# Batch-wide softmax steps on ScalarE and GpSimd, with the maximum and the reciprocal halved on VectorE

## The chip, the cores and the metric

The kernel runs on one core of a Trainium2 chip. A core has five engines that run side by side, each in the order of its own queue: TensorE (PE in the profile, its weight loads PEld), VectorE (DVE), ScalarE (ACT), GpSimd (POOL) and SyncE (SP), which issues the DMAs. The metric is the device time of one execution in microseconds (us); lower is better.

## What is computed

Every token has 8 heads with 7 taps each. A softmax over the 7 taps weighs 7 neighbouring rows of x; the result feeds a feed-forward layer whose activation is h·cos(h).

```python
w = weight_gen - np.max(weight_gen, axis=-1, keepdims=True)
w = np.exp(w)
w = w / (np.sum(w, axis=-1, keepdims=True) + 1e-09)
out = np.einsum('bshk,bskhg->bshg', w, x_unf)      # 8 x 4096 tokens, 192 wide
h = out.reshape(B * S, D) @ w_in                    # 192 -> 2048
return (h * np.cos(h)) @ w_out                      # 2048 -> 192
```

## The kernel before

**Tiling.** A partition holds 256 consecutive tokens (rows). A batch is 4 rows on each of 128 partitions, 512 tokens; there are 64 batches. The 2048 hidden columns are cut into 16 chunks, and a step of the main loop (line 678) handles a pair of chunks of one batch: 8 pairs to a batch, 512 pairs in all, counted by `i`. One softmax (line 263) covers 16 rows, four batches, so it recurs every 32 pairs. I call these 32 pairs a round, and the place in it `p` = i mod 32.

**One pair.** TensorE computes `h` (lines 428 and 445) and, eight pairs behind, the second layer into `acc` (line 519). The cosine goes back and forth: ScalarE L455 rounds `h` to whole turns, VectorE L459 takes the fraction, ScalarE L463 takes the sine, VectorE L466 forms h·cos(h), ScalarE L473 and VectorE L477 split it into a high and a low part for TensorE. There are three `h` buffers; L477 is the last reader of one. `acc` has one buffer. ScalarE empties it with L541 every fourth pair (p = 3, 7, 11, ...), and copies transposed rows out of it with L535 and L536 two pairs from there (p = 1, 5, 9, ...). In every even pair ScalarE also converts transposed rows (L385), and GpSimd finishes them with L387 and L390.

**GpSimd's other work.** For each batch `attention` (line 331) multiplies and adds the seven neighbours: L344 makes a product, L359 adds it to `xa`. Its steps run ahead in the background, two a pair. TensorE transposes the finished `xa` two batches before it is needed, from p = 6, 14, 22 and 30 on (L407). L550 adds the two halves of an output.

**The softmax.** `softmax(..., early=False)` is a generator; line 750 advances it one step at the end of each pair, starting at p = 9 with the load of the taps. VectorE finds the maximum (L276, p = 10); GpSimd subtracts and clips (L278, L285, p = 11). `powers` (line 196) then forms the exponential without ScalarE's exponential table, and does it in two halves of 448 elements a partition: ten ScalarE instructions (L206, twice L214, L224, L228, each for two halves) at p = 14, 15 and in each of p = 18 to 25, and twelve GpSimd instructions (L209 and L211; L217, L219 and L221; L231). At p = 27 GpSimd sums the taps (L190, L193, L297), at p = 29 VectorE takes the reciprocal (L303), and at p = 30 GpSimd multiplies (L309).

**What sets the order.** Each engine's order is the order in which the code emits instructions; nothing reorders them. The tile framework adds the waits between engines.

Of the kernel before, what the change touches and what calls it, by code (L numbers as in the profile page):

```python
# [11 lines left out]
F32 = mybir.dt.float32  # L12
# [4 lines left out]
AF = mybir.ActivationFunctionType  # L17
ALU = mybir.AluOpType
AX = mybir.AxisListType
# [26 lines left out]
LN_2 = math.log(2.0)  # L46
ONE_BITS = float(127 * 2 ** 23)
# [3 lines left out]
def tile_softmax_conv_then_cos_ffn(  # L51
# [8 lines left out]
    nc = tc.nc  # L60
# [36 lines left out]
    early = const.tile([P, 1], F32, name="early")  # L97
# [89 lines left out]
    def add_taps(t, out):  # L187
        three_ = work.tile([P, RW * H, K], F32, name="side", bufs=1)
        three = three_[:, 0:t.shape[1], 0:3]
        nc.gpsimd.tensor_tensor(out=three, in0=t[:, :, 0:3], in1=t[:, :, 3:6], op=ALU.add)  # L190
        old = three[:, :, 0]
        for more in (three[:, :, 1], three[:, :, 2], t[:, :, 6]):
            nc.gpsimd.tensor_tensor(out=out, in0=old, in1=more, op=ALU.add)  # L193
            old = out

    def powers(t):

        (a1, b1), (a2, b2) = EXP_A
        n = t.shape[1]
        whole_ = work.tile([P, RW * H, K], I32, name="whole", bufs=1)  # L200
        side_ = work.tile([P, RW * H, K], F32, name="side", bufs=1)
        cut = (slice(0, n // 2), slice(n // 2, n))
        t, whole, side = ([v[:, c] for c in cut] for v in (t, whole_, side_))

        def near(k):
            nc.scalar.activation(out=whole[k], in_=t[k], func=AF.Identity, scale=1.0 / LN_2)  # L206

        def rest(k):
            nc.gpsimd.tensor_scalar(  # L209
                out=side[k], in0=whole[k], scalar1=-LN_2, scalar2=1.0, op0=ALU.mult, op1=ALU.mult)  # L210
            nc.gpsimd.tensor_tensor(out=t[k], in0=side[k], in1=t[k], op=ALU.add)  # L211

        def square(k, to, a):
            nc.scalar.activation(out=to[k], in_=t[k], func=AF.Square, bias=a, scale=0.5)  # L214

        def quartic(k):
            nc.gpsimd.tensor_scalar(  # L217
                out=side[k], in0=side[k], scalar1=b1, scalar2=1.0, op0=ALU.add, op1=ALU.mult)
            nc.gpsimd.tensor_scalar(  # L219
                out=t[k], in0=t[k], scalar1=b2, scalar2=1.0, op0=ALU.add, op1=ALU.mult)  # L220
            nc.gpsimd.tensor_tensor(out=t[k], in0=t[k], in1=side[k], op=ALU.mult)  # L221

        def power(k):
            nc.scalar.activation(  # L224
                out=whole[k], in_=whole[k], func=AF.Relu, bias=ONE_BITS, scale=2.0 ** 23)

        def again(k):
            nc.scalar.activation(out=t[k], in_=t[k], func=AF.Square)  # L228

        def product(k):  # L230
            nc.gpsimd.tensor_tensor(out=t[k], in0=t[k], in1=whole[k].bitcast(F32), op=ALU.mult)  # L231

        near(0)
        yield
        near(1)
        rest(0)
        yield
        rest(1)
        yield
        yield  # L240
        square(0, side, a1)
        yield
        square(0, t, a2)
        yield
        square(1, side, a1)
        quartic(0)
        yield
        square(1, t, a2)
        yield
        power(0)  # L250
        quartic(1)
        yield
        power(1)
        yield
        again(0)
        yield
        again(1)
        product(0)
        yield
        product(1)  # L260
        yield

    def softmax(r0, r1, eng, early=True, to=None):
        n = (r1 - r0) * H
        if r0 == 0:
            t = const.tile([P, n, K], F32, name="taps0")
        else:
            tile_ = work.tile([P, RW * H, K], F32, name="taps")
            t = tile_[:, 0:n, :]
        nc.sync.dma_start(out=t.rearrange("p a k -> p (a k)"), in_=g_v[:, :, r0 * H * K:r1 * H * K])  # L270
        for b in range(r0 // R, r1 // R):
            taps[b] = t.rearrange("p (r h) k -> p r h k", h=H)[:, b * R - r0:(b + 1) * R - r0]
        yield
        top_ = work.tile([P, RW * H], F32, name="top", bufs=1)
        top = top_[:, 0:n]
        nc.vector.tensor_reduce(out=top, in_=t, axis=AX.X, op=ALU.max)  # L276
        yield
        eng.tensor_tensor(  # L278
            out=t, in0=t, in1=top.unsqueeze(2).broadcast_to([P, n, K]), op=ALU.subtract)
        if early:  # L280
            yield
            nc.scalar.activation(out=t, in_=t, func=AF.Exp)
            yield
        else:
            eng.tensor_scalar(  # L285
                out=t, in0=t, scalar1=0.0, scalar2=EXP_LEAST, op0=ALU.min, op1=ALU.max)
# [10 lines left out]
        (nc.vector if early else nc.gpsimd).tensor_scalar(  # L297
            out=den, in0=den, scalar1=1e-9 / (1.0 if early else EXP_UNIT), scalar2=TWO_PI,
            op0=ALU.add, op1=ALU.mult)
        yield  # L300
        if not early:
            yield
        nc.vector.reciprocal(out=den, in_=den)  # L303
        yield
        m = 0 if to is None else to.shape[1]
        if m:
            eng.tensor_tensor(
                out=to, in0=t[:, 0:m], in1=den[:, 0:m].unsqueeze(2).broadcast_to([P, m, K]), op=ALU.mult)
        eng.tensor_tensor(  # L309
            out=t[:, m:], in0=t[:, m:], in1=den[:, m:].unsqueeze(2).broadcast_to([P, n - m, K]),  # L310
            op=ALU.mult)
        ready.update(range(r0 // R, r1 // R))
# [80 lines left out]
    def transpose_all(b):  # L393
        xa = mixed[b]
        tr = ps_h.tile([P, 2, CT], F32, name="h")
        for part in range(2):
            for r in range(R):
                nc.tensor.transpose(tr[:, part, r * P:(r + 1) * P], xa[:, r, columns(part)], ident)
        transposed.add(b)
        return tr  # L400
# [207 lines left out]
    own = own.rearrange("p a b -> p (a b)")  # L608
    own_taps = own[:, 0:RV * H * K].rearrange("p (n k) -> p n k", k=K)
    sm0 = softmax(0, R, nc.vector, to=own_taps)  # L610
    next(sm0)
    load_rows(0)
    w_b0 = w_in_b(0)
    w_a0 = w_in_a(0, 256)
    sm1 = softmax(R, 3 * R, nc.gpsimd)
    next(sm1)
    load_rows(1)
    w_a1 = w_in_a(256, 768)
    sm2 = softmax(3 * R, 3 * R + RW, nc.gpsimd)
    next(sm2)  # L620
    load_weights(-1)
# [56 lines left out]
    for i in range(N + LAG + 1):  # L678
# [48 lines left out]
        if whole is not None:  # L727
            t = work.tile([P, 2, CT], F32, name="part", bufs=2)
# [65 lines left out]
```

## Time and profile before

| | us |
|---|---|
| median of 3 runs (lowest, highest) | 2228.36 (2226.72, 2228.66) |
| profiled execution, its own time | 2226.02 |
| profiled execution, span from first to last instruction | 2224.2 |
| DVE busy | 1900.0 (85%) |
| ACT busy | 1869.2 (84%) |
| POOL busy | 2015.8 (91%) |

A group row of the profile reads: line, engine, operation, output<-inputs, shapes (partitions x elements), count, then busy time in us and the mean of one in ns, then the idle time of the engine ahead of it and what ended that. A timeline row reads: start in us from the span's start, duration in us, engine, line, operation; where the engine stood idle ahead of it, that time and its releaser follow in brackets. A wait row reads: who waited for whom, total us, how often, longest us. A row of the windows reads: stretch, its length, then busy us of PE, PEld, DVE, ACT and POOL with instruction counts, then the granted TensorE clock.

### The profile page before, as it was taken

What the parts mean: (1) busy time and instruction counts of PE and PEld (TensorE: products, weight loads), DVE (VectorE), ACT (ScalarE), POOL (GpSimd) and SP (SyncE); (2) the same over time, 40 slices, a digit from 0 to 9 for tenths busy, and PEclk for the clock granted to TensorE, in tenths of its full rate; (3) what the DMA queues carried; (4) which work ended last, traced back from release to release, by engine and by line L of the source; (5) the groups of instructions that cost most, each with busy time, mean ns of one, the idle gap of its engine ahead of it and who ended that gap; (6) DMA issues with size and microseconds to landing.
All of it is one profiled execution on the core that took longest, in us unless ns stands there. A gap on an engine that the chain in (4) does not pass through costs nothing.

```text
span 2224.2 us, 62220 instructions
## 1 busy us (share of the span) xinstructions
PE 2160.8 (97%) x26552; PEld 1677.8 (75%) x26552; DVE 1900.0 (85%) x1638; ACT 1869.2 (84%) x2352; POOL 2015.8 (91%) x1778
## 2 busy tenths in 40 slices
PE   5699999999999999999999999999999999999998
PEld 3477777777777777777777777777777777777777
DVE  6888888888888888888888888888888888888886
ACT  4688888988888898888988888888888988888885
POOL 8999999999999999999999999999999999989830
PEclk7899999999999999999999999999999999999999
DMA  7221221221221221211211221211212112212100
GB/s 176 49 48 34 56 48 38 51 48 39 51 56 30 59 48 30 60 43 43 52 42 45 48 50 39 56 42 40 56 34 56 48 34 56 48 36 48 30 16 19
DMA packets 53285, 105.67 MB, mean 48 GB/s; under 512 B 5791, under 2 KB 42135, under 8 KB 53007
## 3 DMA queue, kind: packets, MB, share of 16 engines
q1 hardware_dynamic: 53006, 101.69, 19.2%
q8 instruction: 208, 3.41, 0.7%
q14 instruction: 71, 0.57, 0.1%
HBM read 76.50 MB, written 25.17 MB: 46 GB/s over the span
## 4 chain that ended last, share of the span: by engine, by line
PE 55%; POOL 40%; issue 2%; ACT 1%; DVE 1%; DMA 0%; POOLq 0%; SPq 0%; ACTq 0%; DVEq 0%
PE acc L519 27%; PE h L445 17%; POOL xa L359 14%; POOL pr L344 11%; PE h L428 9%; POOL x_lo L390 3%; POOL part L550 2%; POOL taps L211 1%; POOL taps L221 1%; POOL taps L231 1%; POOL x_b L387 1%; POOL xa L344 1%; POOL den L193 1%; PE acc L407 1%; POOL side L209 1%
## 5 line engine op out<-in xcount | busy, mean ns | idle before, releaser
L459 DVE TENSOR_TENSOR turn<-h,turn 128x1024 f32<-128x1024 f32 x512 | 625.7, 1222 | 275.8 <-ACT turn L455 275.2
L519 PE MATMUL acc<-wo,ghi 64*128 64x384 f32 x8096 | 805.9, 336 | 1.8 <-DVE t L149 1.5
L519 PEld LDWEIGHTS acc<-wo,ghi 64*128 64x128 f32 x8096 | 724.5, 184 | 55.2 <-ACT part L541 10.8
L463 ACT ACTIVATE turn<-turn 128x1024 f32<-128x1024 f32 x512 | 541.7, 1058 | 216.3 <-DVE turn L459 216.3
L359 POOL TENSOR_TENSOR xa<-xa,pr 128x768 f32<-128x768 f32 (+1 forms) x384 | 698.6, 1819 | 1.7
L466 DVE SCALAR_TENSOR_TENSOR h<-h,turn 128x1024 f32<-128x1024 f32 x512 | 630.8, 1232 | 2.5 <-ACT turn L463 2.5
L477 DVE TENSOR_TENSOR glo<-h,ghi 128x1024 bf16<-128x1024 f32 x512 | 621.3, 1214 | 1.1 <-ACT ghi L473 1.1
L455 ACT ACTIVATE turn<-h 128x1024 int32<-128x1024 f32 x512 | 523.6, 1023 | 84.9 <-PE h L445 76.2
L344 POOL TENSOR_TENSOR pr<-xt,taps 128x768 f32<-128x768 f32 (+1 forms) x384 | 588.2, 1532 | 5.2
L473 ACT CAST ghi<-h 128x1024 fp32r<-128x1024 f32 x512 | 516.6, 1009 | 2.9 <-DVE h L466 1.3
L519 PE MATMUL acc<-wo_b,glo 64*128 64x192 bf16 x8096 | 462.5, 243 | 0.1
L519 PEld LDWEIGHTS <-glo 64*128 64x128 bf16 (+1 forms) x8128 | 318.1, 94 | 85.8 <-issue 67.7
L428 PE MATMUL h<-x_hi,wa_hi 64*128 64x512 f32 x1024 | 300.8, 583 | 0.0
L445 PE MATMUL h<-x_hi,wa_hi 64*128 64x512 f32 x1024 | 299.9, 582 | 0.0
L428 PE MATMUL h<-x_lo,wa_hi 64*128 64x512 bf16 x1024 | 199.0, 384 | 31.6 <-DVE glo L477 23.5
L445 PE MATMUL h<-x_hi,wb_hi 64*128 64x512 f32 x1024 | 204.2, 395 | 0.0
L428 PE MATMUL h<-x_b,wa_lo 64*128 64x512 bf16 x1024 | 196.7, 380 | 3.5 <-POOL wa_lo L155 3.5
L445 PE MATMUL h<-x_lo,wa_hi 64*128 64x512 bf16 x1024 | 196.0, 379 | 0.8
L445 PE MATMUL h<-x_b,wa_lo 64*128 64x512 bf16 x1024 | 196.2, 379 | 0.0
L445 PE MATMUL h<-x_lo,wb_hi 64*128 64x512 bf16 x1024 | 195.8, 379 | 0.0
L445 PE MATMUL h<-x_b,wb_lo 64*128 64x512 bf16 x1024 | 195.8, 378 | 0.0
L387 POOL TENSOR_SCALAR x_b<-x_hi 128x256 bf16<-128x256 f32 (+1 forms) x247 | 103.6, 420 | 93.0 <-ACT x_hi L385 90.6
(87 smaller groups left out, 2000.3 us busy)
## 6 DMA issues: line engine op xcount, KB each, us to landing
xt<-in_x_dram SPq DMA_DIRECT2D x62, 960.0 KB, 7.0
out_dram<-part SPq DMA_DIRECT2D x256, 96.0 KB, 2.2
taps<-in_weight_gen_dram SPq DMA_DIRECT2D x15, 448.0 KB, 4.5
raw<-in_moe_w_out_dram SPq DMA_DIRECT2D x8, 384.0 KB, 12.2
raw<-in_moe_w_in_dram SPq DMA_DIRECT2D x10, 256.0 KB, 11.1
xt<-in_x_dram SPq DMA_DIRECT2D x1, 768.0 KB, 10.0
xt<-in_x_dram SPq DMA_DIRECT2D x1, 540.0 KB, 5.5
raw<-in_moe_w_in_dram SPq DMA_DIRECT2D x4, 128.0 KB, 9.8
```

The source lines that it names most:

```text
L344: eng.tensor_tensor(out=dst.rearrange("p r (h g) -> p r h g", h=H), in0=xt[:, k + ra:k + rb, :].rearrange("p r (h g) -> p r h g", h=H), in ...
L359: eng.tensor_tensor(out=acc if k < K else xa, in0=acc, in1=old[:, ra:rb], op=ALU.add)
L387: nc.gpsimd.tensor_scalar(out=near[:, :, cs], in0=hi[:, :, cs].bitcast(F32), scalar1=1.0, scalar2=1.0, op0=ALU.mult, op1=ALU.mult)
L428: nc.tensor.matmul(h[:, q, :], lhsT=w[rs, chunk(pair, q)], rhs=v[rs, q, :], start=(m == 0), stop=False, skip_group_check=True)
L445: nc.tensor.matmul(h[:, 1 - q, :], lhsT=w[rs, cs], rhs=v[rs, q ^ middle, :], start=False, stop=(m == len(prods) - 1), skip_group_check=True)
L455: nc.scalar.activation(out=t.bitcast(I32), in_=hs[i], func=AF.Identity, bias=0.25, scale=1.0)
L459: nc.vector.tensor_tensor(out=t, in0=hs[i], in1=t.bitcast(I32), op=ALU.subtract)
L463: nc.scalar.activation(out=t, in_=t, func=AF.Sin, bias=SIN_BIAS, scale=SIN_SCALE)
L466: nc.vector.scalar_tensor_tensor(out=hs[i], in0=hs[i], scalar=TWO_PI, in1=turns.pop(i), op0=ALU.mult, op1=ALU.mult)
L473: nc.scalar.copy(out=hi, in_=hs[i])
L477: nc.vector.tensor_tensor(out=lo, in0=hs.pop(i), in1=hi.bitcast(F32), op=ALU.subtract)
L519: nc.tensor.matmul(to, lhsT=g[rs, n, t * P:(t + 1) * P], rhs=w[rs, fc, :], start=(lo == 0 and c == 0 and (k == 0 or whole and k == 1)), st ...
```

## The change

The halves in `powers` go: each of the five ScalarE and six GpSimd steps now handles all 896 elements in one instruction. ScalarE's steps stand at p = 14, 18, 20, 22 and 26, all even; empty steps (`wait`) keep them there. The maximum becomes two instructions, the first at p = 10 and the second at p = 11, just ahead of the subtraction. The sums move from p = 27 to p = 28. The reciprocal becomes two instructions at p = 30 and 31, and the multiplication stands at p = 32, which is p = 0 of the next round. The three startup softmaxes (`early=True`) keep one maximum and one reciprocal.

```diff
-        cut = (slice(0, n // 2), slice(n // 2, n))
-        t, whole, side = ([v[:, c] for c in cut] for v in (t, whole_, side_))
...
-        near(0)
-        yield
-        near(1)
-        rest(0)
-        yield
-        rest(1)
-        yield
-        yield
-        square(0, side, a1)
-        yield
-        square(0, t, a2)
-        yield
-        square(1, side, a1)
-        quartic(0)
...
+        whole, side = (v[:, 0:t.shape[1]] for v in (whole_, side_))
+        nc.scalar.activation(out=whole, in_=t, func=AF.Identity, scale=1.0 / LN_2)
+        yield
+        nc.gpsimd.tensor_scalar(
+            out=side, in0=whole, scalar1=-LN_2, scalar2=1.0, op0=ALU.mult, op1=ALU.mult)
+        nc.gpsimd.tensor_tensor(out=t, in0=side, in1=t, op=ALU.add)
+        yield
+        yield from wait(2)
+        nc.scalar.activation(out=side, in_=t, func=AF.Square, bias=a1, scale=0.5)
+        yield
+        yield from wait(1)
+        nc.scalar.activation(out=t, in_=t, func=AF.Square, bias=a2, scale=0.5)
...
+        nc.scalar.activation(out=whole, in_=whole, func=AF.Relu, bias=ONE_BITS, scale=2.0 ** 23)
+        nc.gpsimd.tensor_tensor(out=t, in0=t, in1=side, op=ALU.mult)
+        yield
+        yield from wait(3)
+        nc.scalar.activation(out=t, in_=t, func=AF.Square)
+        yield
+        nc.gpsimd.tensor_tensor(out=t, in0=t, in1=whole.bitcast(F32), op=ALU.mult)
...
-        nc.vector.tensor_reduce(out=top, in_=t, axis=AX.X, op=ALU.max)
-        yield
+        cut = (slice(0, n),) if early else (slice(0, n // 2), slice(n // 2, n))
+        for c in cut:
+            nc.vector.tensor_reduce(out=top[:, c], in_=t[:, c], axis=AX.X, op=ALU.max)
+            if early or c.start == 0:
+                yield
...
-        nc.vector.reciprocal(out=den, in_=den)
-        yield
+        for c in cut:
+            nc.vector.reciprocal(out=den[:, c], in_=den[:, c])
+            yield
```

The order on TensorE and SyncE stays as it was, so the DMAs do too. Lines from 303 on move up by 27 (L455 is L428 in the new file, L541 is L514), those between by 28 or 29.

The first place is ScalarE's queue at p = 18 to 20 of a round in the middle of the program. Before, one half-width step follows in every pair (`side` and `taps` are the operands of the exponential, `x_hi` the transposed rows, `part<-acc` the emptying of `acc`):

```order
L385 CAST x_hi<-xrow 128x2x128
L214 ACTIVATE side<-taps 128x448
L455 ACTIVATE turn<-h 128x1024
L473 CAST ghi<-h 128x1024
L463 ACTIVATE turn<-turn 128x1024
L541 COPY part<-acc 128x1024
L214 ACTIVATE taps<-taps 128x448
L455 ACTIVATE turn<-h 128x1024
L473 CAST ghi<-h 128x1024
L463 ACTIVATE turn<-turn 128x1024
L385 CAST x_hi<-part 128x2x128
L214 ACTIVATE side<-taps 128x448
```

After the change the same stretch holds two full-width steps:

```order
L358 CAST x_hi<-xrow 128x2x128
L213 ACTIVATE side<-taps 128x896
L428 ACTIVATE turn<-h 128x1024
L446 CAST ghi<-h 128x1024
L436 ACTIVATE turn<-turn 128x1024
L514 COPY part<-acc 128x1024
L428 ACTIVATE turn<-h 128x1024
L446 CAST ghi<-h 128x1024
L436 ACTIVATE turn<-turn 128x1024
L358 CAST x_hi<-part 128x2x128
L216 ACTIVATE taps<-taps 128x896
```

The step behind the copy out of `acc` is gone, and the step behind each conversion `x_hi` is twice as wide.

The second place is GpSimd's queue at p = 25 to 28, where `xa` for the transposes at p = 30 is finished. Before, five instructions of the sums stand ahead of the last addition to `xa`:

```order
L231 TENSOR_TENSOR taps<-taps,whole 128x448
L344 TENSOR_TENSOR pr<-xt,taps 128x768
L359 TENSOR_TENSOR xa<-xa,pr 128x768
L550 TENSOR_TENSOR part<-part 128x2x192
L190 TENSOR_TENSOR side<-taps 128x128x3
L193 TENSOR_TENSOR den<-side 128x128
L193 TENSOR_TENSOR den<-den,side 128x128
L193 TENSOR_TENSOR den<-den,taps 128x128
L297 TENSOR_SCALAR den<-den 128x128
L359 TENSOR_TENSOR xa<-xa,pr 128x768
L387 TENSOR_SCALAR x_b<-x_hi 128x2x128
L390 TENSOR_TENSOR x_lo<-part,x_hi 128x2x128
```

After the change:

```order
L317 TENSOR_TENSOR pr<-xt,taps 128x768
L332 TENSOR_TENSOR xa<-xa,pr 128x768
L523 TENSOR_TENSOR part<-part 128x2x192
L229 TENSOR_TENSOR taps<-taps,whole 128x896
L332 TENSOR_TENSOR xa<-xa,pr 128x768
L360 TENSOR_SCALAR x_b<-x_hi 128x2x128
L363 TENSOR_TENSOR x_lo<-part,x_hi 128x2x128
L190 TENSOR_TENSOR side<-taps 128x128x3
L193 TENSOR_TENSOR den<-side 128x128
L193 TENSOR_TENSOR den<-den,side 128x128
L193 TENSOR_TENSOR den<-den,taps 128x128
L269 TENSOR_SCALAR den<-den 128x128
```

The last addition (the second L332) and the split of the converted rows now stand ahead of the sums, and one full-width product stands where two halves were spread over two pairs.

The third place is VectorE's queue at p = 10 to 12. Before, one maximum of 128 results stands between two pairs:

```order
L466 SCALAR_TENSOR_TENSOR h<-h,turn 128x1024
L276 TENSOR_REDUCE top<-taps 128x128
L459 TENSOR_TENSOR turn<-h,turn 128x1024
L477 TENSOR_TENSOR glo<-h,ghi 128x1024
L466 SCALAR_TENSOR_TENSOR h<-h,turn 128x1024
L459 TENSOR_TENSOR turn<-h,turn 128x1024
```

After the change:

```order
L439 SCALAR_TENSOR_TENSOR h<-h,turn 128x1024
L247 TENSOR_REDUCE top<-taps 128x64
L432 TENSOR_TENSOR turn<-h,turn 128x1024
L450 TENSOR_TENSOR glo<-h,ghi 128x1024
L439 SCALAR_TENSOR_TENSOR h<-h,turn 128x1024
L247 TENSOR_REDUCE top<-taps 128x64
L432 TENSOR_TENSOR turn<-h,turn 128x1024
```

Each half stands behind the L439 of its own pair; the reciprocal is divided in the same way at p = 30 and 31.

More of the change, by code (lines that the diff above doesn't have):

```diff
@@ L198, in powers @@
         (a1, b1), (a2, b2) = EXP_A
-        n = t.shape[1]
         whole_ = work.tile([P, RW * H, K], I32, name="whole", bufs=1)
         side_ = work.tile([P, RW * H, K], F32, name="side", bufs=1)
-        cut = (slice(0, n // 2), slice(n // 2, n))
-        t, whole, side = ([v[:, c] for c in cut] for v in (t, whole_, side_))
[L205 to L231, printed above, removed]
-        near(0)
+        whole, side = (v[:, 0:t.shape[1]] for v in (whole_, side_))
+        def wait(n):
+            return [None] * n
+        nc.scalar.activation(out=whole, in_=t, func=AF.Identity, scale=1.0 / LN_2)
         yield
-        near(1)
-        rest(0)
+        nc.gpsimd.tensor_scalar(
+            out=side, in0=whole, scalar1=-LN_2, scalar2=1.0, op0=ALU.mult, op1=ALU.mult)
@@ L237, in powers @@
+        nc.gpsimd.tensor_tensor(out=t, in0=side, in1=t, op=ALU.add)
         yield
-        rest(1)
+        yield from wait(2)
+        nc.scalar.activation(out=side, in_=t, func=AF.Square, bias=a1, scale=0.5)
         yield
+        yield from wait(1)
+        nc.scalar.activation(out=t, in_=t, func=AF.Square, bias=a2, scale=0.5)
         yield
-        square(0, side, a1)
+        nc.gpsimd.tensor_scalar(
+            out=side, in0=side, scalar1=b1, scalar2=1.0, op0=ALU.add, op1=ALU.mult)
+        nc.gpsimd.tensor_scalar(
+            out=t, in0=t, scalar1=b2, scalar2=1.0, op0=ALU.add, op1=ALU.mult)
@@ L242, in powers @@
         yield
-        square(0, t, a2)
+        nc.scalar.activation(out=whole, in_=whole, func=AF.Relu, bias=ONE_BITS, scale=2.0 ** 23)
+        nc.gpsimd.tensor_tensor(out=t, in0=t, in1=side, op=ALU.mult)
         yield
-        square(1, side, a1)
-        quartic(0)
+        yield from wait(3)
+        nc.scalar.activation(out=t, in_=t, func=AF.Square)
         yield
-        square(1, t, a2)
-        yield
-        power(0)
-        quartic(1)
-        yield
-        power(1)
-        yield
@@ L255, in powers @@
-        again(0)
-        yield
-        again(1)
-        product(0)
-        yield
-        product(1)
+        nc.gpsimd.tensor_tensor(out=t, in0=t, in1=whole.bitcast(F32), op=ALU.mult)
         yield
```

## The prediction

> **What bounds the kernel now.** I read the page first, then the windows by round, then the waits, then TensorE's timeline pair by pair.
>
> ```profile
> PE 2160.8 (97%) x26552; PEld 1677.8 (75%) x26552; DVE 1900.0 (85%) x1638; ACT 1869.2 (84%) x2352; POOL 2015.8 (91%) x1778
> ...
> 263.09:398.48 135.39, 133.57 (x1668) 104.41 (x1666) 116.23 (x99) 116.06 (x147) 127.98 (x114) 1.00 0.19 46
> ...
> 934.92:1069.04 134.12, 133.24 (x1668) 103.78 (x1666) 116.27 (x99) 116.06 (x147) 127.70 (x114) 1.00 0.19 46
> ...
> PE acc L407 <- POOL xa L359: 9.8, 12, 0.9
> ...
> DVE den L303 <- POOL den L297: 11.7, 14, 3.9
> ```
>
> TensorE is busy for 97% of the span and for 133.24 of the 134.12 us of a round, so only its stalls can be won. The last two rows are waits by which the softmax holds others up: 12 times TensorE waits for the last addition to `xa`, and 14 times the reciprocal waits for the sums. Busy time hides shorter stalls, so I measure those by when each pair's first L445 begins:
>
> ```profile
> 945.31 0.38 PE L445 MATMUL h<-x_lo,wa_hi 64*128 64x512 bf16 x2
> ...
> 961.85 0.38 PE L445 MATMUL h<-x_lo,wa_hi 64*128 64x512 bf16 x2
> ...
> 966.42 0.38 PE L445 MATMUL h<-x_lo,wa_hi 64*128 64x512 bf16 x2
> ...
> 970.56 0.38 PE L445 MATMUL h<-x_lo,wa_hi 64*128 64x512 bf16 x2
> ...
> 974.86 0.38 PE L445 MATMUL h<-x_lo,wa_hi 64*128 64x512 bf16 x2
> ...
> 987.29 0.38 PE L445 MATMUL h<-x_lo,wa_hi 64*128 64x512 bf16 x2
> ...
> 992.43 0.38 PE L445 MATMUL h<-x_lo,wa_hi 64*128 64x512 bf16 x2
> ...
> 1000.71 0.38 PE L445 MATMUL h<-x_lo,wa_hi 64*128 64x512 bf16 x2
> ...
> 1042.04 0.38 PE L445 MATMUL h<-x_lo,wa_hi 64*128 64x512 bf16 x2
> ...
> 1046.18 0.38 PE L445 MATMUL h<-x_lo,wa_hi 64*128 64x512 bf16 x2
> ...
> 1050.48 0.38 PE L445 MATMUL h<-x_lo,wa_hi 64*128 64x512 bf16 x2
> ```
>
> In order these are p = 19, 23, 24, 25, 26, 29, 30, 0, 10, 11 and 12. From 1000.71 to 1042.04 lie ten pairs: 4.133 us a pair undisturbed, 132.26 a round. Above it stand p 23 to 24 (4.57: 0.44 too long), 25 to 26 (4.30: 0.17), 29 to 30 (5.14: 1.01) and 11 to 12 (4.30: 0.17). They sum to 1.79, nearly all of 134.12 - 132.26 = 1.86. So four stalls are the whole reserve of a round, 1.4%.
>
> **The stalls that come from ScalarE.** Its timeline:
>
> ```profile
> 945.99 0.99 ACT L541 COPY part<-acc 128x1024 f32<-128x1024 f32 x1
> ...
> 947.36 1.02 ACT L455 ACTIVATE turn<-h 128x1024 int32<-128x1024 f32 x1
> ...
> 950.93 0.57 ACT L214 ACTIVATE side<-taps 128x448 f32<-128x448 f32 x1
> 951.41 1.01 ACT L455 ACTIVATE turn<-h 128x1024 int32<-128x1024 f32 x1
> ...
> 955.84 1.01 ACT L455 ACTIVATE turn<-h 128x1024 int32<-128x1024 f32 x1
> ...
> 963.14 0.99 ACT L541 COPY part<-acc 128x1024 f32<-128x1024 f32 x1
> ...
> 976.55 1.02 ACT L455 ACTIVATE turn<-h 128x1024 int32<-128x1024 f32 x1
> ...
> 980.72 1.03 ACT L455 ACTIVATE turn<-h 128x1024 int32<-128x1024 f32 x1
> ...
> 1047.20 0.99 ACT L541 COPY part<-acc 128x1024 f32<-128x1024 f32 x1
> ```
>
> From one L455 to the next is ScalarE's loop for a pair, with its round trip over VectorE. An even pair with L385 and a half step takes 951.41 - 947.36 = 4.05; an odd pair with L535, L536 and a half 955.84 - 951.41 = 4.43; an odd pair with L541 alone 980.72 - 976.55 = 4.17. A half step itself takes 0.48 of this (950.93 to 951.41), so L535 and L536 alone leave 3.95. Against TensorE's 4.13, eight pairs in a row with half steps make ScalarE later and later. What that costs is seen at L541, which must empty `acc`. At p = 19 it ends 1.67 after that pair's L445 (946.98 - 945.31) and nobody waits; at p = 11, 2.01 after, the stall is 0.17; at p = 23, 2.28 after, it is 0.44. So **L541 may be 0.17 late; what goes beyond it stalls TensorE in full**. Without L541 more is allowed: at p = 21 ScalarE is 0.4 late and nothing waits.
>
> **The change, part by part.**
>
> ```profile
> L214 ACT ACTIVATE side<-taps 128x448 f32<-128x448 f32 x28 | 16.1, 574 | 0.0
> ...
> L282 ACT ACTIVATE taps<-taps 128x896 f32<-128x896 f32 x1 | 0.9, 950 | 3.2 <-POOL taps L278 3.2
> ...
> L276 DVE TENSOR_REDUCE top<-taps 128x128 f32<-128x896 f32 x15 | 16.1, 1076 | 0.0
> ...
> L276 DVE TENSOR_REDUCE top<-taps 128x64 f32<-128x448 f32 x1 | 0.6, 614 | 0.0
> ...
> L221 POOL TENSOR_TENSOR taps<-taps,side 128x448 f32<-128x448 f32 x28 | 32.2, 1149 | 2.3
> ...
> L278 POOL TENSOR_TENSOR taps<-taps,top 128x896 f32<-128x896 f32 x15 | 26.5, 1764 | 0.0
> ...
> L209 POOL TENSOR_SCALAR side<-whole 128x448 f32<-128x448 int32 x28 | 15.8, 566 | 2.1
> ...
> L285 POOL TENSOR_SCALAR taps<-taps 128x896 f32<-128x896 f32 x14 | 13.1, 936 | 1.2
> ```
>
> *ScalarE.* A full step of another function takes 0.950, 0.38 more than a half, so an even pair with one takes 4.05 + 0.38 = 4.43 and puts ScalarE 0.29 behind. Full steps stand at p = 14, 18, 20, 22, 26; L541 follows at p = 15, 19, 23, 27. Step by step: at 15, 0.29 late, stall 0.12. At 19 the same, 0.12; 0.17 of lateness is left, the L541 there adds 0.04, and the step at p = 20 makes it 0.50 at p = 21, which I take as free under the wider limit (at most 0.1). The pair with L535 and L536 gives back 0.18; the step at p = 22 makes 0.61 at p = 23, stall 0.44. At 27, 0.12. Sum **0.80 a round, against 0.44 + 0.17 = 0.61 before**: ScalarE does less work and stalls TensorE more, since every full step stands right ahead of an L541 or of the pair before one. If the delay spreads, it is 0.2 (all below the wider limit); if a full step costs 0.1 more than that row, 1.2.
>
> The Trainium skill, in "Perfetto Trace Analysis", section "Optimizing Scalar/DVE Operations", says that where ScalarE isn't saturated but causes bubbles on other engines, breaking up instructions may let work complete sooner. That speaks against this part, and ScalarE at 84% is such a case; by the rows above it costs 0.19 a round, and the sum would be 19.5 without it.
>
> *Maximum.* The whole one (1.076) made L541 at p = 11 late by 0.34, so VectorE has about 0.7 spare in such a pair. A half takes 0.614: the stall of **0.17 goes**. GpSimd's subtraction, behind L550, which itself waits for L541, finds the second half about done; I count nothing.
>
> *Sums behind the last addition.* GpSimd at the end of a round:
>
> ```profile
> 986.58 0.91 POOL L190 TENSOR_TENSOR side<-taps 128x384 f32<-128x384 f32 x1
> ...
> 989.78 1.83 POOL L359 TENSOR_TENSOR xa<-xa,pr 128x768 f32<-128x768 f32 x1
> ...
> 996.02 0.73 POOL L390 TENSOR_TENSOR x_lo<-xrow,x_hi 128x256 bf16<-128x256 f32 x1
> ...
> 997.91 0.39 PE L428 MATMUL h<-x_lo,wa_hi 64*128 64x512 bf16 x2
> ```
>
> The sums fill 3.20 us (986.58 to 989.78) ahead of the addition that TensorE waits for. Behind it, they no longer delay it, so it comes 3.2 us sooner, and the stall at p = 30 needs only 1.01: **it goes**, with two us over. Merged halves help: three one-input steps save 2 x 0.566 - 0.936 = 0.20 each; a full product isn't in the trace, and lies between 1.76 (L278, one operand broadcast) and 2.30 (two halves of L221); I take 2.30, the same form. What is late next on GpSimd is the split of the row converted at p = 30: it ends at 996.75 and its reader L428 starts at 997.91, 1.2 us of cover. Its place in the order is kept, TensorE comes about 1.0 earlier, GpSimd 0.6 (0.20 three times) and six short gaps: some 0.9 us of cover stay.
>
> *Reciprocal.* In the first two rounds GpSimd lags, and VectorE's queue stands still behind the reciprocal:
>
> ```profile
> 184.88 0.95 DVE L303 RECIPROCAL den<-den 128x128 f32<-128x128 f32 x1 [3.85 <-POOL den L297]
> ...
> 188.10 0.39 PE L428 MATMUL h<-x_lo,wa_hi 64*128 64x512 bf16 x2 [1.68 <-DVE glo L477]
> ...
> 191.75 0.39 PE L428 MATMUL h<-x_lo,wa_hi 64*128 64x512 bf16 x2 [1.14 <-DVE glo L477]
> ```
>
> L459 and L477 queue behind it, and TensorE waits 2.82 for L477. Now it stands one pair (4.13) later, more than the 3.85, while the sums end at about the same time: one product half, the addition and the split swap places with them. A half takes between half of 0.95 and 0.95, inside the 0.7 of a pair at the lower end; I take 0.5 and no cost, at most 0.25 a half. So round 1 loses 2.8 of stall, round 2 what it has above a steady round (135.39 - 134.12 = 1.27) besides its 1.0.
>
> **Sum.** A steady round saves 1.01 + 0.17 + 0.61 - 0.80 = 0.99; twelve (the count of the waits for `xa`) make 11.9. Round 1: 2.8 - 0.2 = 2.6. Round 2: 0.99 + 1.27 = 2.3. Together **16.8 us**. From the profiled execution's own 2226.0 (span 2224.2 and 1.8 around it) that is 2209.2; from the median 2228.4, 2211.6. I say 2210. Startup, the last two rounds without a softmax of this size, and the DMAs keep their time.
>
> **The rivals.**
> 1. *ScalarE's delay fades.* Less work on ScalarE (five steps of 0.95 for ten of 0.574, 1.0 us a round) tells, and the limit at L541 is as wide as at p = 21: 0.2 of stall instead of 0.8. For it: the limit rests on three places only. 14 rounds of 0.6 more: 2202. The same section of the Trainium skill says that grouping into larger operations can improve throughput where the engine is saturated; at 84% that isn't plainly the case here.
> 2. *A new wait eats part.* The split for p = 32 comes late, or a half reciprocal delays L541 at p = 31, by 0.3 to 1 a round: 2214 to 2224, say 2218. Against it: 0.9 us of cover.
> 3. *The early rounds' wait becomes every round's; slower.* The sums now stand behind the last addition and a split. If full products took much longer than two halves, they would end after VectorE's queue has come to the reciprocal. It now comes there less than 0.6 ahead of 989.7 (14 waits sum to 11.7, and one of them is 3.85), so a pair later it comes at about 993.4. The sums I expect at 989.8 + 1.8 for the addition + 1.1 for the split (its second part is the row at 996.02) - 0.9 = 991.8. From 1.6 us later than that VectorE waits, and each further us goes to TensorE less about 1 (3.85 gave 2.8). A round's gain of 1.2 (16.8 in 14 rounds) is used up at about 1.6 + 1 + 1.2 = 3.8 us late, from which point this rival decides; 5.6 late cost 3 a round, 14 x 3 - 17 = 25 slower, 2226 + 25 = 2251. Only three products of over 3.5 us each would do that, where two halves take 2.30.
> 4. *Nothing shows*: `xa`'s stall goes but every other place fills, within 4.5 us of before.
>
> **How the numbers follow.** Forecast 0.55, rival 1 0.15, rival 2 0.15, rival 3 0.07, rival 4 0.08. A measurement can tell 0.2% (4.5 us) from no change. Faster by more: the forecast, rival 1 and nearly all of rival 2, 0.84; same 0.09; slower 0.07. The range 2200 to 2221 holds forecast and rival 1 (0.70) and two thirds of rival 2. The unknown prices lie in it: ScalarE's 0.2 to 1.2 a round gives -8 to +6, two half reciprocals at 0.25 each +7.
>
> **What would show it.** L407 no longer waits for `xa` and VectorE's waits for the sums vanish. The pairs 11 to 12, 25 to 26 and 29 to 30 fall to 4.13. Pairs 15, 19 and 27 show 0.1, and p 23 to 24 about 0.4, with ScalarE's emptying of `acc` as releaser. A steady round takes 133.1. A round above 134 or a wait of VectorE for the sums would prove me wrong; stalls at 15, 19 and 27 that are absent, or twice the size, would mean that the limit at L541 is misread.

## The result and the profile after

| | before | after |
|---|---|---|
| median of 4 runs each, us | 2227.86 | 2209.26 |
| lowest to highest | 2226.72 to 2228.66 | 2208.66 to 2210.26 |
| profiled execution, span | 2224.2 | 2207.0 |

The changed kernel takes 0.9917 of the time before (95% interval 0.9905 to 0.993), 18.6 us less by the medians and 17.2 less between the two profiled spans.

First the page's busy times after, then its chain of work that ended last, then the windows of one round in the middle of the program (stretch, length, busy us of PE, PEld, DVE, ACT and POOL, granted clock, DMA share, GB/s):

```profile
PE 2157.4 (98%) x26552; PEld 1680.2 (76%) x26552; DVE 1905.9 (86%) x1668; ACT 1861.8 (84%) x2277; POOL 2001.9 (91%) x1688
...
PE 96%; POOL 1%; DVE 1%; ACT 1%; DMA 0%; issue 0%; SPq 0%; DVEq 0%; ACTq 0%; POOLq 0%
...
857.74:990.81 133.07, 133.07 (x1670) 105.14 (x1666) 116.60 (x101) 115.53 (x142) 126.80 (x107) 1.00 0.20 47
```

The same line of the chain before:

```profile
PE 55%; POOL 40%; issue 2%; ACT 1%; DVE 1%; DMA 0%; POOLq 0%; SPq 0%; ACTq 0%; DVEq 0%
```

GpSimd has left the chain: 40% of it before, 1% now, although it is as busy as before (91%). The busy shares hardly differ; what went is time in which one engine stood still for another. A steady round takes 133.07 us instead of 134.12. In the windows PE's busy time fills all 133.07, and still 0.8 of it is stall: stalls this short don't show there and have to be taken from the distances between pairs, as in the prediction.

Here are those distances, the start of each pair's first L418 (L445 before) on TensorE's timeline after, for p = 15, 16, 23, 24, 29 and 30 of that round:

```profile
919.75 0.39 PE L418 MATMUL h<-x_lo,wa_hi 64*128 64x512 bf16 x2
...
924.00 0.38 PE L418 MATMUL h<-x_lo,wa_hi 64*128 64x512 bf16 x2
...
953.15 0.38 PE L418 MATMUL h<-x_lo,wa_hi 64*128 64x512 bf16 x2
...
957.63 0.38 PE L418 MATMUL h<-x_lo,wa_hi 64*128 64x512 bf16 x2
...
978.42 0.39 PE L418 MATMUL h<-x_lo,wa_hi 64*128 64x512 bf16 x2
...
982.55 0.39 PE L418 MATMUL h<-x_lo,wa_hi 64*128 64x512 bf16 x2
```

Against 4.13 undisturbed, p 15 to 16 takes 4.25 (0.12 more), p 23 to 24 takes 4.48 (0.35 more), and p 29 to 30 takes 4.13: the stall of 1.01 for `xa` is gone. The whole round:

| excess over 4.133 us behind p = | 11 | 15 | 19 | 21 | 23 | 25 | 27 | 29 | sum | round |
|---|---|---|---|---|---|---|---|---|---|---|
| before | 0.17 | | | | 0.44 | 0.17 | | 1.01 | 1.79 | 134.12 |
| after | | 0.12 | 0.12 | 0.09 | 0.35 | | 0.12 | | 0.80 | 133.07 |

**Where the 17.2 us came from.** Twelve steady rounds fall from 134.11 on average to 133.07, 12.5 us. The second round falls from 135.39 to 133.06, 2.3. The first loses 2.8: its stalls of 1.87 and 1.50 behind p = 30 and 31 are gone, one behind p = 15 is 0.7 longer than before, and the small ones behind p = 19 to 27 sum to about what they did. Against that, the main loop began 0.5 us later in this execution (over all the kernels below, this start varies by up to 1.1 us). 12.5 + 2.3 + 2.8 - 0.5 = 17.1.

The waits for the softmax are gone with them. Of the rows of the view of waits (who waited for whom, total us, how often, longest) on which the prediction stood, neither TensorE's for `xa` nor VectorE's for the sums appears any more; what has grown is the wait for ScalarE's emptying of `acc`. After, then before:

```profile
PEld acc L492 <- ACT part L514: 16.4, 57, 0.6
```

```profile
PEld acc L519 <- ACT part L541: 10.8, 32, 0.5
```

57 such waits instead of 32: four copies out of `acc` in a round now come late, where two did before. The 5.6 us more, 0.4 a round, are not the price. The view counts what a weight load waited, and by the distances the stalls of ScalarE's grew from 0.61 to 0.80; experiment 2 puts the price of merging at 0.15 a round.

### The profile page after: what moved, and what is told of

Same layout as the page of the kernel before. It is cut to its first block, busy times and chain, and to the rows that moved or that the text cites. A ratio compares the mean times of both kernels' runs of the same rounds, so it can differ in the third digit from the quotient of the medians.

```text
span 2207.0 us, 62098 instructions
## 1 busy us (share of the span) xinstructions
PE 2157.4 (98%) x26552; PEld 1680.2 (76%) x26552; DVE 1905.9 (86%) x1668; ACT 1861.8 (84%) x2277; POOL 2001.9 (91%) x1688
## 3 DMA queue, kind: packets, MB, share of 16 engines
q1 hardware_dynamic: 53006, 101.69, 19.3%
## 4 chain that ended last, share of the span: by engine, by line
PE 96%; POOL 1%; DVE 1%; ACT 1%; DMA 0%; issue 0%; SPq 0%; DVEq 0%; ACTq 0%; POOLq 0%
PE acc L492 48%; PE h L418 30%; PE h L401 15%; PE acc L380 1%; PE h L604 1%; POOL xa L332 0%; POOL pr L317 0%; PE h L492 0%; DMA xt<-in_x_dram 0%; DVE glo L450 0%; DVE turn L432 0%; DVE x_lo L363 0%; POOL wa_lo L155 0%; ACT turn L428 0%; POOL xa L317 0%
## 5 line engine op out<-in xcount | busy, mean ns | idle before, releaser
L332 POOL TENSOR_TENSOR xa<-xa,pr 128x768 f32<-128x768 f32 (+1 forms) x384 | 699.9, 1823 | 0.7
L439 DVE SCALAR_TENSOR_TENSOR h<-h,turn 128x1024 f32<-128x1024 f32 x512 | 631.3, 1233 | 2.5 <-ACT turn L436 2.5
L428 ACT ACTIVATE turn<-h 128x1024 int32<-128x1024 f32 x512 | 524.7, 1025 | 90.7 <-PE h L418 80.9
L401 PE MATMUL h<-x_hi,wa_hi 64*128 64x512 f32 x1024 | 300.8, 583 | 0.0
L418 PE MATMUL h<-x_hi,wa_hi 64*128 64x512 f32 x1024 | 300.1, 582 | 0.0
L401 PE MATMUL h<-x_lo,wa_hi 64*128 64x512 bf16 x1024 | 199.2, 384 | 26.8 <-DVE glo L450 19.9
L418 PE MATMUL h<-x_hi,wb_hi 64*128 64x512 f32 x1024 | 204.5, 395 | 0.0
L401 PE MATMUL h<-x_b,wa_lo 64*128 64x512 bf16 x1024 | 196.8, 380 | 3.6 <-POOL wa_lo L155 3.6
L418 PE MATMUL h<-x_lo,wa_hi 64*128 64x512 bf16 x1024 | 196.3, 379 | 0.8
L418 PE MATMUL h<-x_b,wa_lo 64*128 64x512 bf16 x1024 | 196.2, 379 | 0.0
L418 PE MATMUL h<-x_lo,wb_hi 64*128 64x512 bf16 x1024 | 196.1, 378 | 0.0
L418 PE MATMUL h<-x_b,wb_lo 64*128 64x512 bf16 x1024 | 195.9, 378 | 0.0
```

The lines of the kernel that those rows point to most:

```text
L332: eng.tensor_tensor(out=acc if k < K else xa, in0=acc, in1=old[:, ra:rb], op=ALU.add)
L401: nc.tensor.matmul(h[:, q, :], lhsT=w[rs, chunk(pair, q)], rhs=v[rs, q, :], start=(m == 0), stop=False, skip_group_check=True)
L418: nc.tensor.matmul(h[:, 1 - q, :], lhsT=w[rs, cs], rhs=v[rs, q ^ middle, :], start=False, stop=(m == len(prods) - 1), skip_group_check=True)
L428: nc.scalar.activation(out=t.bitcast(I32), in_=hs[i], func=AF.Identity, bias=0.25, scale=1.0)
L439: nc.vector.scalar_tensor_tensor(out=hs[i], in0=hs[i], scalar=TWO_PI, in1=turns.pop(i), op0=ALU.mult, op1=ALU.mult)
```

## The experiments

The change does four things at once: it moves the sums and the reciprocal, halves the maximum, halves the reciprocal, and merges the half steps. My theory was the prediction's: the order on GpSimd removes the stall for `xa`, the halved maximum the 0.17, the distance of two pairs keeps VectorE from waiting, and merging on ScalarE costs time. Rivals were that merging on GpSimd is what frees `xa`, that the merged ScalarE steps help, and that halving or the distance does nothing. All ratios are against the kernel before, which had a median of 2226.86 us beside experiments 1, 2, 3 and 7 and 2226.63 beside 4, 5, 6 and 8.

| kernel | median us | ratio, interval | steady round | stalls left in it |
|---|---|---|---|---|
| 1: sums one pair later, nothing else | 2210.65 | 0.9927 (0.9912 to 0.9942) | 133.10 | 0.17 at 11, 0.45 at 23, 0.17 at 25 |
| 2: experiment 1 and both halvings | 2208.37 | 0.9915 (0.99 to 0.993) | 132.92 | 0.44 at 23, 0.18 at 25 |
| 3: changed, sums back ahead of the addition | 2209.47 | 0.9919 (0.9904 to 0.9934) | 133.04 | as changed |
| 4: changed, whole maximum | 2210.86 | 0.993 (0.9911 to 0.995) | 133.20 | as changed, and 0.17 at 11 |
| 5: changed, whole reciprocal | 2208.22 | 0.9919 (0.9899 to 0.9938) | 133.03 | as changed |
| 6: changed, reciprocal one pair behind the sums | 2228.85 | 1.0011 (1.0 to 1.0021) | 134.42 | as changed, and 1.38 at 31 |
| 7: changed, ScalarE's steps every fourth pair | 2201.73 | 0.9883 (0.9867 to 0.99) | 132.31 | none |
| 8: experiment 7, first round as changed | 2199.02 | 0.9878 (0.9862 to 0.9895) | 132.31 | none |

Differences of a few tenths of a us in a round are read from the traces, where the rounds of one kernel agree within 0.05 us from the fifth on; the medians of kernels 1 to 5 lie too close together for their intervals to tell them apart.

### 1. Only the place of the sums

```diff
+            yield
             add_taps(t, den)
```

This is the kernel before, with the sums (and so everything behind them) one pair later. The reciprocal stays whole, the steps of `powers` stay in halves.

> The kernel before with one empty step ahead of the sums: they stand at p = 28 behind the last addition to xa, the whole reciprocal at p = 30, the multiplication at p = 31. ScalarE and GpSimd keep their halves, the maximum stays whole. Theory (the place of the sums takes the stall at p = 30 and the early waits of the reciprocal): those vanish; left are 0.61 of ScalarE's stalls, 0.17 of the maximum and about 0.05 of the whole reciprocal: a round of 133.1, a span of 2207 (before 2224.2). Rival (the merged steps on GpSimd are needed): the stall at p = 30 stays at 0.5 to 1.0, a round of 133.6 to 134.1, a span of 2214 to 2221.

Steady rounds of 133.10 instead of 134.11: the stall for `xa` is gone, the other three stand where they stood. GpSimd's last addition and its reader on TensorE (an L408 here), from their timelines:

```profile
980.87 1.83 POOL L360 TENSOR_TENSOR xa<-xa,pr 128x768 f32<-128x768 f32 x1
```

```profile
984.97 0.22 PE L408 MATMUL acc<-ident,xa 64*128 64x64 f32 x2
```

The addition ends at 982.70, 2.3 us ahead of its reader: the "two us over" of the prediction. The span of 2210.4 was some 3 us above what I expected (the other three executions of this kernel were 1.5 us shorter). In this one the main loop began 1.1 us later than in that of before, and stalls of 1.70 in the first round and 0.53 in the second stayed, behind p = 31. TensorE's timeline names what it waits for there (first round), and GpSimd's shows it:

```profile
192.00 0.39 PE L429 MATMUL h<-x_lo,wa_hi 64*128 64x512 bf16 x2 [1.55 <-POOL x_lo L391]
```

```profile
191.23 0.73 POOL L391 TENSOR_TENSOR x_lo<-xrow,x_hi 128x256 bf16<-128x256 f32 x1
```

It is the split of the converted row for p = 32, which the prediction called next in line to be late.

### 2. The place and the halves, without merging

```diff
-        nc.vector.tensor_reduce(out=top, in_=t, axis=AX.X, op=ALU.max)
-        yield
+        cut = (slice(0, n),) if early else (slice(0, n // 2), slice(n // 2, n))
+        for c in cut:
+            nc.vector.tensor_reduce(out=top[:, c], in_=t[:, c], axis=AX.X, op=ALU.max)
+            if early or c.start == 0:
+                yield
...
+            yield
             add_taps(t, den)
...
-        nc.vector.reciprocal(out=den, in_=den)
-        yield
+        for c in cut:
+            nc.vector.reciprocal(out=den[:, c], in_=den[:, c])
+            yield
```

> The same with maximum and reciprocal in two halves: the change without its merged steps. Theory (full steps on ScalarE stall TensorE more than the ten halves): left are 0.61 a round, 132.88, a span of about 2204.5, that is 2 to 3 us below the changed kernel's 2207.0. Rival (merging helps): 2207 or more, with a stall at p = 30 or more than 0.77 of ScalarE's stalls.

This is the change without the merged steps. One round of it in the windows:

```profile
858.40:991.32 132.92, 132.84 (x1668) 104.25 (x1666) 116.55 (x101) 116.10 (x147) 127.80 (x113) 1.00 0.20 47
```

132.92 is 0.15 less than the changed kernel's 133.07, with stalls of 0.44 + 0.18 against 0.80. So merging costs time in a steady round, as the prediction had it (0.19 a round). In the whole program this isn't seen: the span is 2206.4 against 2207.0, where 12 x 0.15 = 1.8 less was due. Without merging, the first two rounds kept stalls of 0.77 and 0.52 behind p = 31, which the changed kernel doesn't have. They are waits for the same split of GpSimd's as in experiment 1, here in the first round:

```profile
190.48 0.39 PE L433 MATMUL h<-x_lo,wa_hi 64*128 64x512 bf16 x2 [0.63 <-POOL x_lo L395]
```

So merging does help through GpSimd, which then catches up sooner: 1.3 us of the 1.8 are given back in these two rounds.

### 3. The sums ahead of the addition again

```diff
         nc.gpsimd.tensor_tensor(out=t, in0=t, in1=whole.bitcast(F32), op=ALU.mult)
-        yield
...
         if not early:
             yield
+            yield
```

From here on the changed kernel is the base. The sums go back to p = 27, ahead of the last addition to `xa`; the second added line keeps the reciprocal at p = 30 and 31.

> The changed kernel with the sums back at p = 27, ahead of the last addition to xa, straight behind the product; the reciprocals stay at p = 30 and 31. In the changed kernel that addition ends 3.6 us before its reader, and the sums take 3.2. Theory A (merging on GpSimd alone would have been enough): no stall at p = 30, 0.4 of cover left, a round of 133.07, a span of 2207. Theory B (the place of the sums is needed, as the prediction had it): the stall at p = 30 comes back with 0.1 to 1.0 a round, a span of 2208 to 2221.

No stall came back. GpSimd's timeline and the reader on TensorE's:

```profile
973.67 2.12 POOL L229 TENSOR_TENSOR taps<-taps,whole 128x896 f32<-128x896 f32 x1
975.87 0.93 POOL L190 TENSOR_TENSOR side<-taps 128x384 f32<-128x384 f32 x1
...
978.65 0.30 POOL L268 TENSOR_SCALAR den<-den 128x128 f32<-128x128 f32 x1
979.03 1.85 POOL L332 TENSOR_TENSOR xa<-xa,pr 128x768 f32<-128x768 f32 x1
```

```profile
981.21 0.22 PE L380 MATMUL acc<-ident,xa 64*128 64x64 f32 x2
```

The sums delay the addition by 3.2 us as they did before, and it ends at 980.88, just 0.33 ahead of its reader. With half steps it came 1.01 too late. ScalarE's steps are merged here too, but the instructions ahead of the addition are GpSimd's: by the group rows of the kernel before and of the changed one its six steps save some 0.19 each (an L209 pair 2 x 0.566 against 0.941, an L231 pair 2 x 1.164 against 2.123), 1.1 of the 1.34 between the two. So moving the sums (experiment 1) and merging the steps (this one) each remove that stall alone. The prediction gave it all to the place of the sums.

### 4. The whole maximum

```diff
-        for c in cut:
-            nc.vector.tensor_reduce(out=top[:, c], in_=t[:, c], axis=AX.X, op=ALU.max)
-            if early or c.start == 0:
-                yield
+        nc.vector.tensor_reduce(out=top, in_=t, axis=AX.X, op=ALU.max)
+        yield
```

> The changed kernel with the maximum whole again at p = 10. Theory (the whole maximum makes the emptying of acc at p = 11 late by 0.34, of which 0.17 stalls): the pair 11 to 12 is 0.17 too long again, all others as in the changed kernel, a round of 133.24, a span of 2209. Rival (with GpSimd and ScalarE in other phases the maximum is hidden): no stall there, 2207.

0.17 behind p = 11 is back, and the round is 0.13 to 0.14 longer. The halved maximum is worth this much and no more.

### 5. The whole reciprocal

```diff
-        for c in cut:
-            nc.vector.reciprocal(out=den[:, c], in_=den[:, c])
+        nc.vector.reciprocal(out=den, in_=den)
+        yield
+        if not early:
             yield
```

> The changed kernel with the reciprocal whole at p = 30. It takes 0.95 where the whole maximum takes 1.08, so the emptying of acc at p = 31 is about 0.2 late. Theory (0.17 of it free): 0.0 to 0.1 at the pair 31 to 32, a span of 2207 to 2208. Rival (any whole VectorE step ahead of an emptying of acc costs 0.17 or more): 2209.4 or more.

No stall behind p = 30 or 31, and a round of 133.03 against 133.07. Halving the reciprocal gains nothing at this place.

### 6. The reciprocal one pair behind the sums

```diff
-        if not early:
-            yield
         for c in cut:
             nc.vector.reciprocal(out=den[:, c], in_=den[:, c])
```

> The changed kernel with the reciprocal's halves at p = 29 and 30, one pair behind the sums instead of two, the multiplication at p = 31. In the changed kernel's profile the sums end at 982.4 and VectorE comes to this earlier place at 980.5, so it would wait 1.9 a round. Theory (VectorE's queue standing behind the reciprocal is what costs): the lateness less a cover of about 0.8 reaches TensorE at p = 30 and 31, 1.0 to 1.2 a round, a span of 2221 to 2224, nearly all of the gain lost. Rival (two pairs aren't needed, the wait is hidden): 2207.

The whole gain is lost: the span is 2226.4, above the 2221 to 2224 that I expected. The wait of VectorE in this kernel's view of waits, the first half of the reciprocal on its timeline (in brackets the idle time ahead of it and its releaser), and what TensorE then waits for:

```profile
DVE den L274 <- POOL den L269: 28.0, 14, 2.4
```

```profile
990.89 0.55 DVE L274 RECIPROCAL den<-den 128x64 f32<-128x64 f32 x1 [1.94 <-POOL den L269]
991.36 1.16 DVE L430 TENSOR_TENSOR turn<-h,turn 128x1024 f32<-128x1024 f32 x1
```

```profile
997.69 0.39 PE L399 MATMUL h<-x_lo,wa_hi 64*128 64x512 bf16 x2 [1.02 <-DVE glo L448]
```

In all 14 rounds VectorE stands 2.0 us in front of the reciprocal. What is queued behind it (L430, then the L448 that frees an `h` buffer) comes late, and TensorE loses 1.38. 14 x 1.38 = 19.3, about what lies between the medians (2228.85 - 2209.26 = 19.6). This is the mechanism of the prediction's third rival: with the sums moved by a pair, the reciprocal must move by a pair too, so that two pairs stay between them. Here its first half stands where the whole one stood before, at p = 29.

### 7. ScalarE's steps every fourth pair

```diff
-        yield from wait(1)
+        yield from wait(3)
         nc.scalar.activation(out=t, in_=t, func=AF.Square, bias=a2, scale=0.5)
...
         yield
+        yield from wait(2)
         nc.scalar.activation(out=whole, in_=whole, func=AF.Relu, bias=ONE_BITS, scale=2.0 ** 23)
...
-            yield
-            yield from powers(t)
+            yield from [None] * gap
+            yield from powers(t)
...
-        if i % (SB * NPAIR) == FIRST and b + 6 < NB:
+        if (i == FIRST or i > FIRST and i % (SB * NPAIR) == NPAIR) and b + 6 < NB:
```

If a full step costs something because a copy out of `acc` stands one pair behind it with little slack, then a step in the pair right behind such a copy should cost nothing: three pairs pass before the next. Full steps stand at p = 12, 16, 20, 24 and 28, and the softmax begins one pair earlier to make room (`gap` is 0; in the first round, where the softmax begins at p = 9 as before, it is 3, and the steps stand four pairs later than in the others).

> The changed kernel with ScalarE's five full steps at p = 12, 16, 20, 24 and 28 (the first round at 16 to 32), so that none stands between L385 and the emptying of acc a pair later, but all ahead of the pair with the two small copies. The softmax starts a pair earlier, its end is three pairs later than in the changed kernel. Theory (the emptying of acc may be 0.17 late, other pairs 0.4): each step's 0.29 is free, no stall is left, a round of 132.27, a span of 2196. Rival (a full step's delay reaches TensorE wherever it stands): 0.6 to 0.8 a round as before, a span of 2204 to 2207.

All five stalls are gone, and a steady round is 132.31. But the span is 2202.0 where 2196 was expected: the second round takes 136.58, with a stall of 0.53 behind p = 13 and one of 3.77 behind p = 15. The view of waits names the second, and a row of the windows shows what came behind it:

```profile
PE h L402 <- POOL x_lo L364: 2.1, 1, 2.1
```

```profile
260.00:262.50 2.50, 2.50 (x18) 2.44 (x18) 1.77 (x2) 1.65 (x3) 2.50 (x3) 0.50 0.38 77
```

It is GpSimd's split of a converted row, late once more. The wait is 2.1 of the 3.77. Through the rest TensorE is busy but slow: its granted clock, 1.00 up to 257.5 us, is 0.87 in the 2.5 us from there, 0.50 in the row above and 0.95 in the next 2.5, then 1.00 again. In the first round of the kernel before, with waits of 1.68 and 1.14, it stayed at 1.00. What lowers it no run here isolates. GpSimd has no idle time there, and the first softmax ends six pairs later than in the changed kernel (its last step on ScalarE stands at p = 32 instead of 26); I take this delay as the cause, and the next kernel takes it away.

### 8. The same, but the first round as in the changed kernel

```diff
-        yield from wait(3)
+        yield from wait(1 if gap else 3)
...
-        yield from wait(2)
+        yield from wait(0 if gap else 2)
...
-            yield from [None] * gap
+            if gap:
+                yield
...
-            sm = softmax(r0, min(r0 + RW, RPP), nc.gpsimd, early=False, gap=3 if i == FIRST else 0)
+            sm = softmax(r0, min(r0 + RW, RPP), nc.gpsimd, early=False, gap=1 if i == FIRST else 0)
```

> The changed kernel with ScalarE's five full steps at p = 12, 16, 20, 24 and 28 from the second round on; the first round keeps the places of the changed kernel, since moving it late cost 4.3 us in the second round's start (TensorE waited 2.1 for GpSimd's x_lo there). Theory (only what stands ahead of the emptying of acc is dear): rounds 2 to 14 at 132.3, the first with 0.8 of stalls, a span of 2197 to 2198, 9 to 10 below the changed kernel's 2207.0. Rival (GpSimd is late at the start of the second round whatever the first does): 3 to 4 us of stall there again, a span of 2201.

2199.02 us, 10 us below the changed kernel and 28 below the kernel before: the best of all. One round in the windows; then ScalarE at p = 19 and 20, where L516 is the copy out of `acc`; then TensorE's pairs 19 and 20:

```profile
853.53:985.83 132.30, 132.30 (x1668) 104.14 (x1666) 116.53 (x101) 115.14 (x142) 126.70 (x107) 1.00 0.20 47
```

```profile
932.76 1.00 ACT L516 COPY part<-acc 128x1024 f32<-128x1024 f32 x1
...
937.23 0.95 ACT L216 ACTIVATE taps<-taps 128x896 f32<-128x896 f32 x1
```

```profile
932.08 0.38 PE L420 MATMUL h<-x_lo,wa_hi 64*128 64x512 bf16 x2
...
936.21 0.38 PE L420 MATMUL h<-x_lo,wa_hi 64*128 64x512 bf16 x2
```

The copy ends 1.68 after its pair's L420 (933.76 - 932.08). This is the 1.67 of the undisturbed case in the prediction: in the three pairs between a full step and the next copy ScalarE makes up all its delay. The round lies 0.05 above the undisturbed 132.26. What is left of the kernel's time is TensorE's own work, the startup and the first round's stalls.

## Why the prediction was right

It said 2210, and 2209.26 was measured; the gain by its sum was 16.8 us, and 17.2 lie between the profiled spans. The steps one by one:

**What bounds it.** Right. The stalls were what could be won with TensorE's work as it is, and experiment 8, which removes every one in the steady rounds, ends at the undisturbed pair time that the prediction took as its floor.

**ScalarE's merged steps.** Right in mechanism, place and size. The rule was that the copy out of `acc` may be 0.17 late and that what goes beyond stalls TensorE in full. ScalarE's timeline after, at p = 15 and p = 23:

```profile
920.72 0.99 ACT L514 COPY part<-acc 128x1024 f32<-128x1024 f32 x1
...
954.35 0.99 ACT L514 COPY part<-acc 128x1024 f32<-128x1024 f32 x1
```

At p = 15 it ends 1.96 after that pair's L418 (921.71 - 919.75), 0.29 later than the undisturbed 1.67: exactly the predicted delay, and 0.29 - 0.17 = 0.12 is the stall. At p = 23 it ends 2.19 after, 0.52 late, which gives 0.35. The prediction had 0.61 late and 0.44 there. The stall behind p = 21, put at 0 to 0.1 and entered as nothing, is 0.09, and what TensorE loses there, ScalarE makes up before p = 23. So the sum came out at 0.80 as forecast, with one term 0.09 too large and another 0.09 too small. Rival 1, that the delay fades, is refuted by the same rows, and experiment 2 confirms the sign: without merging a steady round is 0.15 shorter, close to the 0.19. This is also what the rule quoted from the Trainium skill says ("Perfetto Trace Analysis", section "Optimizing Scalar/DVE Operations": smaller instructions where an engine isn't saturated but makes others wait). Experiments 7 and 8 add a condition that the rule doesn't state: full-size steps cost nothing where the instruction that others wait for is three pairs behind them.

**The maximum.** Right: 0.17 gone, and back with the whole maximum (experiment 4).

**The sums behind the last addition.** The stall of 1.01 went, as said. GpSimd's timeline, and the group of the full product:

```profile
974.29 2.13 POOL L229 TENSOR_TENSOR taps<-taps,whole 128x896 f32<-128x896 f32 x1
976.37 1.83 POOL L332 TENSOR_TENSOR xa<-xa,pr 128x768 f32<-128x768 f32 x1
...
979.24 0.91 POOL L190 TENSOR_TENSOR side<-taps 128x384 f32<-128x384 f32 x1
...
982.09 0.30 POOL L269 TENSOR_SCALAR den<-den 128x128 f32<-128x128 f32 x1
...
985.88 0.73 POOL L363 TENSOR_TENSOR x_lo<-xrow,x_hi 128x256 bf16<-128x256 f32 x1
```

```profile
L229 POOL TENSOR_TENSOR taps<-taps,whole 128x896 f32<-128x896 f32 x14 | 29.7, 2123 | 0.0
```

```profile
981.83 0.22 PE L380 MATMUL acc<-ident,xa 64*128 64x64 f32 x2
...
988.02 0.40 PE L401 MATMUL h<-x_lo,wa_hi 64*128 64x512 bf16 x2
```

The addition ends at 978.20, 3.6 us ahead of its reader, where "two us over" was predicted; the split for p = 32 ends at 986.61, 1.4 ahead of its L401, where 0.9 was predicted. The split's cover is larger because a full product takes 2.12, not 2.30 (it lay between the bounds of 1.76 and 2.30, and I took the upper one): three of them make the 0.5. The addition's is larger by all that merging saves, which the prediction named as a help and left out of its two us; without merging they are 2.3 (experiment 1). **What the prediction missed here**: the place of the sums is enough to remove the stall, as it said, but isn't needed. By experiment 3 merging removes it too, with 0.33 us to spare. The changed kernel does both, so the sum wasn't touched.

**The reciprocal.** Right that the two-pair distance is what counts, and that the halves cost nothing there. VectorE after, the two halves:

```profile
984.51 0.54 DVE L276 RECIPROCAL den<-den 128x64 f32<-128x64 f32 x1
...
988.65 0.54 DVE L276 RECIPROCAL den<-den 128x64 f32<-128x64 f32 x1
```

The sums end at 982.39, 2.1 us before VectorE comes (1.6 was expected). The halves take 0.54 (0.5 was taken) and cost nothing; nor does a whole one (experiment 5). Experiment 6 shows the rival that would have made it slower, one pair away: a wait of 2.0 us there costs 1.38 a round. The prediction's conversion, the wait less about 1, gives 1.0 and was too low.

**Early rounds.** 2.6 and 2.3 were predicted, 2.8 and 2.3 measured. That the first comes so close is partly luck. The prediction took away the 2.8 of TensorE's two waits, while by the distances 3.4 went; and it didn't foresee the 0.7 that came in behind p = 15.

**A new wait (rival 2).** It named the split for p = 32. In the changed kernel nobody waits for it; experiments 1 and 2 show that this is owed to the merged steps on GpSimd, without which it stalls the first two rounds.

**Startup keeps its time.** Not quite: one pair early in the first round is 0.7 us longer than before (last section). It is inside the 2.8.

## What to carry to other kernels

Busy shares said nothing here, and ScalarE's work even fell while its stalls grew: measure the distance between successive iterations of the bounding engine, find for each long gap the instruction that came late, and see how much lateness that instruction may have before anyone waits. Merge small steps only where the instructions behind them have room for the longer one; the same merged steps cost 0.8 us a round with four of the five one pair ahead of a copy that TensorE waits for, and nothing with all five right behind one. An instruction that waits for another engine holds up all that is queued behind it, so it belongs far enough behind its producer: here one pair was too near by 2 us, and two pairs left 2 us to spare.

## What the hardware did that I had not expected

Rows of the first round, VectorE and GpSimd at work on the same 1024-wide tile (`x_hi` and its parts), before:

```profile
117.92 1.22 DVE L390 TENSOR_TENSOR x_lo<-part,x_hi 128x1024 bf16<-128x1024 f32 x1
```

```profile
117.94 2.11 POOL L387 TENSOR_SCALAR x_b<-x_hi 128x1024 bf16<-128x1024 f32 x1
```

After:

```profile
118.25 1.97 DVE L363 TENSOR_TENSOR x_lo<-part,x_hi 128x1024 bf16<-128x1024 f32 x1
```

```profile
118.10 1.05 POOL L360 TENSOR_SCALAR x_b<-x_hi 128x1024 bf16<-128x1024 f32 x1
119.11 2.51 POOL L317 TENSOR_TENSOR pr<-xt,taps 128x768 f32<-128x768 f32 x1
```

Whichever starts second is stretched by what is left of the first, less about 0.15. Before, VectorE starts 0.02 earlier and takes 1.22, and GpSimd's split takes 2.11. After, GpSimd starts 0.15 earlier and takes 1.05, and VectorE takes 1.97; GpSimd's next product, which meets the rest of that, takes 2.51 where others of this form near it take 1.53 to 1.56. The Trainium skill has this rule ("SBUF — State Buffer", section "SBUF: two separate sides": a VectorE instruction with two SBUF inputs and a GpSimd one that reads SBUF share a port pair, the first to start holds it for its whole length, and the other waits); these rows agree with it. Soon after, TensorE waits for VectorE:

```profile
122.54 0.39 PE L401 MATMUL h<-x_lo,wa_hi 64*128 64x512 bf16 x2 [0.66 <-DVE glo L450]
```

The other kernels' traces bear on whether this is one chain. In all ten the pair of instructions behaves in one of these two ways. VectorE starts first (by 0.02 or 0.03) in the three with the whole maximum: the kernel before, experiment 1 and experiment 4. GpSimd starts first (by 0.14 or 0.15) in the seven with the halved one; there the stall behind p = 15 is 1.10 to 1.12 and this wait of TensorE's 0.66 or 0.67. Experiment 4 differs from the changed kernel in the maximum alone:

```profile
119.03 1.22 DVE L361 TENSOR_TENSOR x_lo<-part,x_hi 128x1024 bf16<-128x1024 f32 x1
120.58 1.22 DVE L430 TENSOR_TENSOR turn<-h,turn 128x1024 f32<-128x1024 f32 x1 [0.34 <-ACT turn L426]
```

```profile
119.05 2.10 POOL L358 TENSOR_SCALAR x_b<-x_hi 128x1024 bf16<-128x1024 f32 x1
```

```profile
123.00 0.39 PE L399 MATMUL h<-x_lo,wa_hi 64*128 64x512 bf16 x2 [0.34 <-DVE glo L448]
```

TensorE's wait is half as long here and the stall 0.79, and VectorE's own wait behind its L361 is for ScalarE. In the kernel before and in experiment 1, where ScalarE's steps are halves, the stall is 0.41. So the halved maximum turned the order, by 0.17 us, and the order is worth 0.3 with merged steps; with halves the difference is 0.7 (experiment 2's 1.11 against experiment 1's 0.41). How the halves of the maximum turn it stays open.
